# Seven of the K and V loads of a two-layer decode step are issued as three DMAs of 112, 8 and 8 rows

## The chip, the cores and the metric

The kernel runs on one core of a Trainium2 chip. The metric is the device time of one execution in microseconds (us). Of the kernel before, three runs are shown: 294.25, 294.75 and 295.55 us, so the median is 294.75 us. The profiled execution took 293.41 us, and its span in the profile is 291.6 us.

The core has five instruction streams that matter here: TensorE (PE, with its weight loads as PEld), VectorE (DVE), ScalarE (ACT), GpSimd (POOL) and SyncE (SP). SP computes nothing; it issues nearly all the DMAs. The data of a DMA is moved by the core's 16 DMA engines.

## The reference, cut to what matters

Two layers with the same weights and the same K and V caches are applied to four single-token rows `x` (batch 4, width 512, all bf16). Each layer is grouped-query attention followed by a gated MLP, each behind a layer norm without weights and each added to `x`:

```
q = (layernorm(x) @ wq) as 4 x 32 heads x 128          # 8 KV heads, 4 query heads on each
p = softmax(q . k_cache / sqrt(128))                   # k_cache: 4 x 8 x 4096 x 128
x = x + ((p . v_cache) @ wo)
h = sigmoid(layernorm(x) @ w_gate) * (layernorm(x) @ w_up)   # width 1792
x = x + h @ w_down
```

and the same again. K of one batch row and one KV head is 4096 x 128 in bf16, which is 1 MB, and V is the same. One layer reads 32 such K and 32 such V.

## The kernel before, in words

**Units and slots.** The work is cut into units: one layer, one batch row, one KV head. There are 64, and two neighbouring KV heads of one batch row form a pair. The string `ORDER` (line 118) writes out the order of the 32 pairs. The K or the V of a unit goes into a slot, an SBUF tile of 128 partitions with 8 KB in each. There are 14 slots (`NSLOT`), and four more when `wq` is no longer needed: `yield_wq` (line 1134) then gives its space away. Some K and V of the first layer stay in their slots for the second (`KEPT`), so 45 K and 49 V are loaded, each a load of 128 rows (one row for a partition, 8 KB). The last V alone is loaded as two halves of its columns.

**The order of the loads.** The string `LOADS` (line 122) writes out the order of all loads after `wq`, one letter for each: k and v for K and V, o for a piece of `wo`, g, u and d for the weights of the MLP. `loads` (line 333) is made from it, and `pump` (line 364) issues loads from its head on the queue of SP as long as a slot is free. SP waits, before each issue, until the last readers of the slot are done. A load raises the semaphore of its slot (`d0` to `d17`) by 16 when it has landed, and `S.last_write` of the slot's key (`s0` and so on) is what readers wait on.

**The work on a unit.** The string `PROGRAM` (line 126) writes out the order of all steps. `k_turn` (line 1142) transposes a landed K on VectorE in place; `scores` (line 1155) multiplies it with the queries on TensorE; `smax`, `spread_max`, `bias` and `expo` (lines 1187 to 1227) make the softmax; `ptrans` and `copies` turn the probabilities; `pv` (line 1323) multiplies them with V, and frees V's slot; `normalise` divides by the sums. Between the layers each batch row has a chain of 17 small steps (`pass_steps`, line 1088): the projection `wo`, the MLP and the queries of the second layer. After the last unit of the second layer comes the last MLP for all rows, and the output.

**What orders what.** Each engine runs its own list in the order written. Between engines `_Sched` (line 34) sets semaphore waits from the keys that a step reads and writes. A DMA is such a step: its token is counted in the order of the list, so that a wait on a later DMA of the same semaphore covers the earlier ones.

Of the kernel before, what the change touches and what calls it, by code (L numbers as in the profile page):

```python
# [119 lines left out]
111 113 133 131 130 132 122  # L120
"""
LOADS = """
ovkovookkk kkkuvkovkk vkovokovvg guddvkvkvv kkkvvkvvkk vkvvvvkkkv kvkkvkvvkv kvvkvkvkvv kvkvkkkvvk
vkvkvkvvvv kkkvvvvv
"""
PROGRAM = """
szmTbtpt snetzhbtuwmrpnPuiCtuuD sehtPzrtmpnaawtueawb szuatotDCuPiauuhabu
# [12 lines left out]
def bass_interleave_layers__gqa_block_cached__glu_gated_glu__decode_kernel(  # L140
# [17 lines left out]
    P = 128  # L158
# [19 lines left out]
    S = _Sched()  # L178
# [4 lines left out]
    def sbt(shape, dtype, name):  # L183
        cnt[0] += 1
        return es.enter_context(nc.sbuf_tensor(f"{name}_{cnt[0]}", list(shape), dtype))
# [27 lines left out]
    slot = [sbt([P, NJ * DH], dt.bfloat16, f"slot{i}") for i in range(NSLOT)]  # L213
# [110 lines left out]
    def loaded(kind, i):  # L324
        return seq[i][0] == 0 or not kept(kind, i)

    queue = {kind: [i for i in range(NU) if loaded(kind, i)] for kind in "kv"}
# [2 lines left out]
    queue["u"] = list(range(KD // 2))  # L330
    queue["d"] = list(range(2))
    kinds = {"k": "k", "v": "v", "o": "wo", "g": "wg", "u": "wu", "d": "wd"}
    loads = [(kinds[c], queue[c].pop(0)) for c in LOADS if not c.isspace()]
    assert not any(queue.values())
    loads.reverse()

# [24 lines left out]
    def take():  # L361
        return free.pop(0)

    def pump():
        while loads:
            kind, n = loads[-1]
            if kind in wparts:
                loads.pop()
                dst, src = wparts[kind](n)
                S.dma("sp", (lambda dst, src: lambda e: e.dma_start(dst, src))(dst, src), f"wo{n}" if kind == "wo" else kind, writes=[f"{kind}{n}"])  # L370
                continue
            if not free:
                return
            loads.pop()
            s = take()
            _, b, u = seq[n]
            if kind == "k":
                where["kn", n] = s
                src = A_k_cache[b, u].rearrange("(p j) d -> p (j d)", p=P)
            else:  # L380
                where["v", b, u] = s
                src = A_v_cache[b, u].rearrange("(p j) d -> p (j d)", p=P)
            parts = [(slot[s][:, :], src, f"d{s}", f"s{s}")]
            if kind == "v" and n == NU - 1:
                h = NJ * DH // 2
                parts = [(slot[s][:, 0:h], src[:, 0:h], "vh", "vh"), (slot[s][:, h:], src[:, h:], f"d{s}", f"s{s}")]
            for dst, frm, sem, key in parts:
                deps = S.readers.get(f"s{s}", []) + [S.last_write.get(f"s{s}")] if key == "vh" else ()
                S.dma(
                    "sp", (lambda dst, frm: lambda e: e.dma_start(dst, frm))(dst, frm), sem, writes=[key], deps=deps  # L390
                )
# [8 lines left out]
    for n in range(KD // 2):  # L400
# [4 lines left out]
            writes=[f"wq{2 * n}", f"wq{2 * n + 1}"],  # L405
        )
    pump()

    S.inst("pool", lambda e: e.memset(qz_sb[:, :, :, :, :], 0.0), writes=QZ + ["pf"])
# [6 lines left out]
        writes=["pe0"],  # L416
    )
    dve(lambda e: e.transpose(pidx[:, :], iota_f[:, 0:32]), writes=["pe0"])
    for a in range(4):
# [6 lines left out]
            writes=[f"ident{a}"],  # L426
# [5 lines left out]
    for k in range(KD):  # L432
# [13 lines left out]
        writes=[f"x{b}" for b in range(Bn)],  # L446
# [1183 lines left out]
    head_masks()  # L1630
    k_turn(0)
    pump()
    k_turn(1)
    pump()
    q_mm(Bn, 0, HQ)
    q_spread(0, Bn)
# [112 lines left out]
    for c in PROGRAM:  # L1749
# [29 lines left out]
        writes=["sel_row"],  # L1779
# [4 lines left out]
        writes=["rowk"],  # L1784
# [3 lines left out]
    for part in range(2):  # L1788
# [21 lines left out]
        writes=["o_row"],  # L1810
# [56 lines left out]
```

## Time and profile before

| | us |
|---|---|
| median of three runs (lowest, highest) | 294.75 (294.25, 295.55) |
| the profiled execution | 293.41 |
| its span in the profile | 291.6 |
| PE busy | 213.6 (73%) |
| DVE busy | 194.1 (67%) |
| ACT busy | 109.3 (37%) |
| POOL busy | 42.3 (15%) |

The span is the time between the first and the last instruction of the profiled execution. The page of the profile gives the busy time of each engine, then the span in 40 equal slices, then the DMA queues: for each queue the packets, the megabytes, and the time that its packets took as a share of 16 engines' span. A packet is one row of a load, or a completion mark of 4 bytes. Further views give the waits (who waited for whom, us in total, times, longest), the chain of work that ended last, the instructions in order of time, and the busy time of the engines in stretches of the span.

### The profile page before, as it was taken

The numbers are of one execution on the slowest core, as the hardware profiler recorded it, in microseconds if no ns is written. First come the engines' busy times: TensorE is split into PE (matmuls) and PEld (weight loads), VectorE is DVE, ScalarE is ACT, GpSimd is POOL, SyncE is SP. The second block draws the span as 40 slices with busy tenths as digits, with TensorE's granted clock in tenths as the row PEclk, the third lists the DMA queues.
The fourth block names the chain that finished last, engine by engine and source line by source line (L and its number), as shares of the span: only waits on it lengthen the run. The fifth ranks groups of instructions, "written<-read, shape, count | busy, mean of one in ns | idle before, by whom it ended". The sixth has DMA issues, their size and how long they took to land. (4 is left out here: it accounts for less than half of the span.)

```text
span 291.6 us, 10424 instructions
## 1 busy us (share of the span) xinstructions
PE 213.6 (73%) x4416; PEld 129.9 (45%) x4416; DVE 194.1 (67%) x498; ACT 109.3 (37%) x357; POOL 42.3 (15%) x213
## 2 busy tenths in 40 slices
PE   1130224666586886889988898999997899887895
PEld 1130101333336452455744454574564556463485
DVE  6420399876344866758789795868779595869443
ACT  2000114135330362653363554434646334566620
POOL 0000112202000121310011321001231200231100
PEclk9999999999997575755777555575555575766655
DMA  7999999999999999999999999999999999999900
GB/s 281 412 403 396 421 422 405 418 405 395 416 397 420 419 417 421 397 411 424 415 423 419 417 415 415 400 402 419 417 421 416 421 411 373 419 424 418 376 11 5
DMA packets 19781, 113.13 MB, mean 388 GB/s; under 512 B 1812, under 2 KB 5912, under 8 KB 7576
## 3 DMA queue, kind: packets, MB, share of 16 engines
q1 hardware_dynamic: 19712, 112.47, 94.5%
q8 instruction: 35, 0.57, 0.8%
q14 instruction: 10, 0.08, 0.1%
q10 hardware_dynamic: 24, 0.01, 0.0%
HBM read 112.46 MB, written 0.00 MB: 386 GB/s over the span
## 5 line engine op out<-in xcount | busy, mean ns | idle before, releaser
L1153 DVE STREAM_TRANSPOSE slot<-slot 128x1024 f32<-128x1024 f32 (+2 forms) x89 | 103.8, 1173 | 24.2 <-DMA slot<-in_A_k_cache_dram 23.3
L1290 ACT ACTIVATE pT<-PT 32x128 bf16<-32x128 f32 x232 | 62.0, 267 | 53.8 <-PE O_ps L1338 20.5
L1170 PE MATMUL S_ps<-slot,qz 128*16 128x512 bf16 x488 | 58.6, 597 | 10.6 <-DVE slot L1153 7.2
L1338 PEld LDWEIGHTS O_ps<-pT,slot 128*128 128x128 bf16 x1696 | 49.9, 102 | 28.5 <-ACT pT L1290 15.5
L1338 PE MATMUL O_ps<-pT,slot 128*128 128x4 bf16 x1696 | 54.1, 166 | 8.4 <-ACT pT L1290 6.8
L795 POOL COPY qz<-qs 32x32 bf16<-32x32 bf16 x112 | 22.8, 203 | 91.5 <-PE S_ps L1170 50.2
L1189 DVE TENSOR_REDUCE small_c<-S_ps 128x1 bf16<-128x512 f32 x32 | 21.7, 678 | 13.5 <-PE S_ps L1170 13.5
L1252 POOL TENSOR_TENSOR small_a<-small_b 128x8 bf16<-128x8 f32 x32 | 6.4, 199 | 137.0 <-ACT wide L1224 127.1
L1224 ACT ACTIVATE wide<-S_ps,small_b 128x512 bf16<-128x512 f32 x20 | 14.1, 705 | 23.3 <-DVE small_b L1217 19.3
L1170 PEld LDWEIGHTS S_ps<-slot,qz 128*16 128x16 bf16 x488 | 11.1, 103 | 26.3 <-issue 11.0
L1235 PE MATMUL PT<-ident_bf,wide 128*128 128x64 bf16 (+1 forms) x288 | 17.8, 221 | 3.4 <-ACT pT L1290 2.4
L1235 PEld LDWEIGHTS PT<-ident_bf,wide 128*128 128x128 bf16 x288 | 14.5, 118 | 8.5 <-issue 3.4
L1224 ACT ACTIVATE wide<-S_ps,small_b,small_a 128x512 bf16<-128x512 f32 x12 | 9.3, 778 | 12.9 <-DVE small_b L1217 5.1
L1399 PE MATMUL AC<-wo,oT 128*1 128x512 bf16 x96 | 11.7, 584 | 2.9 <-DVE oT L1373 2.9
L1197 PE MATMUL O_ps<-ident_bf,small_c 128*128 128x64 bf16 x32 | 7.0, 217 | 8.7 <-DVE small_c L1189 6.3
L747 PE MATMUL M_ps<-t_row,ident_bf 128*32 128x128 bf16 x16 | 0.6, 307 | 15.6 <-DVE t_row L730 15.6
L978 PE MATMUL M_ps<-wq,small_a 128*1 128x512 bf16 (+1 forms) x128 | 11.1, 510 | 0.6 <-DVE small_a L697 0.5
L758 ACT ACTIVATE qs<-M_ps 128x128 bf16<-128x128 f32 x4 | 0.8, 284 | 26.6 <-PE M_ps L747 26.6
L1197 PEld LDWEIGHTS O_ps<-ident_bf,small_c 128*128 128x128 bf16 x32 | 3.3, 104 | 14.9 <-DVE small_c L1189 8.9
L900 PE MATMUL M_ps<-wg,small_a 128*1 128x512 bf16 (+1 forms) x64 | 8.2, 556 | 1.6 <-DVE small_a L537 1.6
L925 PE MATMUL M_ps<-wu,small_a 128*1 128x512 bf16 (+1 forms) x64 | 9.1, 578 | 0.0
L1217 DVE TENSOR_REDUCE small_b<-O_ps 128x1 f32<-128x64 f32 x32 | 7.2, 225 | 2.8
(171 smaller groups left out, 241.6 us busy)
## 6 DMA issues: line engine op xcount, KB each, us to landing
slot<-in_A_v_cache_dram SPq DMA_DIRECT2D x47, 1024.0 KB, 9.8
slot<-in_A_k_cache_dram SPq DMA_DIRECT2D x42, 1024.0 KB, 11.1
wq<-in_A_wq_dram SPq DMA_DIRECT2D x2, 2048.0 KB, 10.2
wo<-in_A_wo_dram SPq DMA_DIRECT2D x8, 512.0 KB, 15.7
wq<-in_A_k_cache_dram SPq DMA_DIRECT2D x3, 1024.0 KB, 13.1
wu<-in_B_w_up_dram SPq DMA_DIRECT2D x2, 896.0 KB, 18.9
wg<-in_B_w_gate_dram SPq DMA_DIRECT2D x2, 896.0 KB, 14.2
wd<-in_B_w_down_dram SPq DMA_DIRECT2D x1, 1024.0 KB, 19.0
```

The costliest lines, as they stand in the source:

```text
L795: (lambda a, ps: lambda e: e.tensor_copy(qz_sb[ps, :, :, a, :], qs_sb[b][ps, :, c0:c0 + 2 * REP].rearrange("p t (u r) -> p u t r", r=REP), ...
L925: (lambda k, st, nt: lambda e: e.matmul(M_ps[1][32 * st:32 * st + 1, 0:nt * 2 * P], lhsT=xc_bf[:, k, 0:1], rhs=wv[:, k, bass.ds(st, nt, st ...
L978: (lambda k, st: lambda e: e.matmul(M[32 * st:32 * st + 1, 0:nj * P], lhsT=xc_bf[:, k, 0:1], rhs=q_rows[:, k, h, j0:j0 + nj, st, :], start ...
L1153: dve(lambda e: e.transpose(kf, kf), writes=[f"s{st}"])
L1170: (lambda t, b2, e_, c, ul, r0, ktv: lambda e: e.matmul(S_ps[p][r0:r0 + 4 * REP, :], lhsT=qz_sb[:, ul, t, :, :].rearrange("p a r -> p (a r)"),
L1189: dve(lambda e: e.tensor_reduce(rm_bf[:, 0:1], S_ps[p][:, :], AX.X, ALU.max), reads=[f"S{p}"], writes=["rmb"])
L1197: lambda e: e.matmul(O_ps[n][:, P:P + 64], lhsT=rm_bf[:, 0:1].broadcast_to([P, P]), rhs=valid_bf, start=True, stop=True),
L1224: lambda e: e.activation(pe_sb, S_ps[p][:, :], ACTF.Exp, bias=nm_sb, scale=scale, accum_out=sm_sb),
L1235: (lambda w, a0, a1, c0: lambda e: e.matmul(PT[:, c0:c0 + 16 * (a1 - a0)], lhsT=wide_sb[:, NV + 64 * w:NV + 64 * w + P], rhs=valid_bf[:, : ...
L1290: (lambda dst, frm: lambda e: e.activation(dst, frm, ACTF.Copy))(dst, frm),
L1338: (lambda n, x, c, j: lambda e: e.matmul(bank[:, ul * REP:(ul + 1) * REP], lhsT=vv[:, x * JG + c * 4 + j, :], rhs=pT[:, x % 2, j, x // 2, ...
L1399: (lambda r, h, i: lambda e: e.matmul(AC[32 * r:32 * r + 1, :], lhsT=oT_sb[:, h, own_column:own_column + 1], rhs=wo_sb[:, h, :], start=(j ...
```

## The change

In `LOADS` seven letters become capitals: three k and four v. They are the letters 43, 55, 64, 73, 84, 94 and 106 of 108. The list `loads` gets a third entry that tells whether the letter was a capital, and `pump` issues such a load as three DMAs on SP, one behind the other: rows 0 to 111, rows 112 to 119 and rows 120 to 127. Only the first of them waits for the slot's earlier readers. All three raise the semaphore of the slot by 16, and the key's last write is the third, so readers wait for all three. The other 87 loads of K and V, the data in the slots, the order of the loads and all other steps stay as they are.

```diff
 LOADS = """
-ovkovookkk kkkuvkovkk vkovokovvg guddvkvkvv kkkvvkvvkk vkvvvvkkkv kvkkvkvvkv kvvkvkvkvv kvkvkkkvvk
-vkvkvkvvvv kkkvvvvv
+ovkovookkk kkkuvkovkk vkovokovvg guddvkvkvv kkKvvkvvkk vkvvVvkkkv kvkKvkvvkv kvVkvkvkvv kvkVkkkvvk
+vkvKvkvvvv kkkvvVvv
 """
@@
-    loads = [(kinds[c], queue[c].pop(0)) for c in LOADS if not c.isspace()]
+    loads = [(kinds[c.lower()], queue[c.lower()].pop(0), c.isupper()) for c in LOADS if not c.isspace()]
@@
-            kind, n = loads[-1]
+            kind, n, uneven = loads[-1]
@@
+            if uneven:
+                whole = None
+                for rows in (slice(0, P - 16), slice(P - 16, P - 8), slice(P - 8, P)):
+                    whole = S.dma(
+                        "sp", (lambda d, f: lambda e: e.dma_start(d, f))(slot[s][rows, :], src[rows, :]), f"d{s}",
+                        writes=() if whole else [f"s{s}"],
+                    )
+                S.last_write[f"s{s}"] = whole
+                continue
```

## The prediction

> **What bounds the kernel now.** I read the page's head, slices and DMA queues first, then the chain, then waits and stretches.
>
> ```profile
> span 291.6 us, 10424 instructions
> PE 213.6 (73%) x4416; PEld 129.9 (45%) x4416; DVE 194.1 (67%) x498; ACT 109.3 (37%) x357; POOL 42.3 (15%) x213
> ...
> DMA  7999999999999999999999999999999999999900
> GB/s 281 412 403 396 421 422 405 418 405 395 416 397 420 419 417 421 397 411 424 415 423 419 417 415 415 400 402 419 417 421 416 421 411 373 419 424 418 376 11 5
> ...
> q1 hardware_dynamic: 19712, 112.47, 94.5%
> q8 instruction: 35, 0.57, 0.8%
> q14 instruction: 10, 0.08, 0.1%
> q10 hardware_dynamic: 24, 0.01, 0.0%
> ```
>
> The DMA engines are full in every slice until 277 us, and no compute engine is. The best slices move about 420 GB/s, so a load of 1.049 MB takes 2.50 us; each of the 16 engines moves 8 of its 128 rows, so a row costs an engine 2.50 / 8 = 0.31 us. Besides the loads there are 35 packets of instructions: 0.8% of 16 x 291.6 us is 37.3 us of one engine's time, 1.07 us a packet.
>
> ```profile
> 229.56 10.75 DMA slot<-in_A_v_cache_dram
> 240.31 0.05 issue
> 240.36 1.00 PE O_ps L1338 x32
> ...
> 249.68 0.33 SPq L390
> 250.00 0.05 issue
> 250.06 11.11 DMA wq<-in_A_k_cache_dram
> 261.16 0.02 issue
> 261.18 2.31 DVE wq L1153
> ```
>
> This is the chain that ended last. It holds two loads, 10.75 and 11.11 us from issue to landing, that is four loads deep in the queue; between and behind them it is compute. Nothing waits for the last load of all: the chain's end is set by when the K load of 250.06 is whole. How close compute runs beside this:
>
> ```profile
> 125.00:180.00 55.00, 48.58 (x992) 28.74 (x984) 41.40 (x108) 26.95 (x88) 9.89 (x49) 0.59 1.01 419
> 180.00:200.00 20.00, 18.93 (x380) 11.54 (x384) 15.55 (x54) 7.38 (x24) 2.61 (x13) 0.59 0.99 401
> 200.00:236.00 36.00, 32.52 (x642) 18.92 (x630) 27.86 (x66) 18.24 (x60) 7.64 (x38) 0.50 1.01 420
> ```
>
> The columns are the stretch, its length, the busy time of PE, PEld, DVE, ACT, POOL, the granted clock and the DMA share. From 200 to 236 us PE is busy for 32.52 of 36 us at a clock of 0.50, beside a DMA share of 1.01. Two resources are nearly full, and the waits between them are short:
>
> ```profile
> PEld O_ps L1338 <- DMA slot<-in_A_v_cache_dram: 0.8, 1, 0.8
> ...
> DVE wq L1153 <- DMA wq<-in_A_k_cache_dram: 1.2, 1, 1.2
> ```
>
> The first is the only wait for a load in 180 to 240 us, the second the longest from 240 us on. They stand where the chain has its two DMA pieces (240.3 and 261.2 us). So an earlier landing is worth at most about 0.8 us at the first, and 1.2 us more at the second, beyond which compute sets the time.
>
> **What the change does to the engines.** It moves rows between DMA engines. How many engines a part uses can be counted from packets and issues:
>
> ```profile
> slot<-in_A_v_cache_dram SPq DMA_DIRECT2D x47, 1024.0 KB, 9.8
> slot<-in_A_k_cache_dram SPq DMA_DIRECT2D x42, 1024.0 KB, 11.1
> wq<-in_A_wq_dram SPq DMA_DIRECT2D x2, 2048.0 KB, 10.2
> wo<-in_A_wo_dram SPq DMA_DIRECT2D x8, 512.0 KB, 15.7
> wq<-in_A_k_cache_dram SPq DMA_DIRECT2D x3, 1024.0 KB, 13.1
> wu<-in_B_w_up_dram SPq DMA_DIRECT2D x2, 896.0 KB, 18.9
> wg<-in_B_w_gate_dram SPq DMA_DIRECT2D x2, 896.0 KB, 14.2
> wd<-in_B_w_down_dram SPq DMA_DIRECT2D x1, 1024.0 KB, 19.0
> wq<-in_A_v_cache_dram SPq DMA_DIRECT2D x1, 1024.0 KB, 8.5
> slot<-in_A_v_cache_dram SPq DMA_DIRECT2D x2, 512.0 KB, 22.8
> wd<-in_B_w_down_dram SPq DMA_DIRECT2D x1, 768.0 KB, 20.5
> out_dram<-slot SPq DMA_DIRECT2D x2, 1.0 KB
> out_dram<-slot ACTq DMA_DIRECT2D x2, 1.0 KB
> t_row<-in_A_x_dram ACTq DMA_DIRECT2D x1, 4.0 KB
> ```
>
> ACT's queue q10 carries three DMAs of 4 rows (x, two quarters of the output): 12 rows, but 24 packets, so each left 4 completion marks, one for each engine used. SP's queue q1 carries 111 loads over 128 partitions and two quarters of the output. Their contiguous pieces are 12,160 (K and V), 256 (wq), 4,096 (wo), 512 (wu, wg), 896 (wd) and 8: 17,928. The other 19,712 - 17,928 = 1,784 packets are marks: 16 for each load, 4 for each quarter. So 4 rows use 4 engines and 128 rows use 16. Of 8 rows the trace has no example; between these rows they use 8, one row on each. Then 112 rows put 7 rows on each of 16 engines, and the two parts of 8 rows put 2 more on the same eight: 9 rows on eight engines, 7 on the others, where it was 8 and 8. Seven such loads move 7 x 0.31 = 2.2 us of work from each of eight engines to each of the other eight. Bytes in all stay the same.
>
> [...]
>
> **Who has room.** A load is whole when its slowest engine is done. If the 37.3 us of instruction packets fell evenly on 16 engines (2.3 us each), the rows would be even now and the change would make them uneven. If they fall on eight engines, these carry 37.3 / 8 = 4.7 us more than the rest; over the span they are the late ones, and the moved work closes 2 x 2.2 = 4.4 of the 4.7 us. Call s the share of the packets on the eight engines that lose rows. The slowest set gets lighter only if s x 4.7 exceeds (1 - s) x 4.7 + 2.2, that is s above 0.73. The trace's completion marks, which no view prints one by one, show the engines of most loads in two sets of eight, an early and a late one, and instruction packets hitting the late set in turn. I take it that the set is eight. That it is the set which loses rows no row says, and the 0.23 below stands for that.
>
> **The sum.** At a DMA share of 0.99 to 1.01 the late engines hardly run dry, so what is taken from them counts in full until compute binds. By count of letters, the V load at 229.56 us is the 93rd, with five split loads ahead of it; the K load at 250.06 us is the 101st, with six.
>
> - First DMA piece: the late engines finish 5 x 0.31 = 1.55 us earlier; the wait there was 0.8 us, so the chain gains 0.8 us and compute binds.
> - Second piece: issue comes 0.8 us earlier. The late engines are 6 x 0.31 = 1.86 us ahead, and DVE, which waited 1.2 us, is free 0.8 us earlier: 2.0 us is there to gain, 1.86 us is taken.
> - Behind it, 30 us of compute shift as they are. The last V, with seven split loads up to it, comes 2.2 us earlier, so no new wait appears.
>
> Together -1.86 us. Against that, what is added:
>
> ```profile
> 229.56 0.33 SPq L390 DMA_DIRECT2D slot<-in_A_v_cache_dram  x1
> 229.94 0.43 SPq L390 DMA_DIRECT2D slot<-in_A_k_cache_dram  x1
> ...
> SPq L106 <- PE O_ps L1338: 94.5, 33, 8.0
> SPq L106 <- PE S_ps L1170: 34.0, 10, 6.0
> ```
>
> Fourteen more issues at 0.33 to 0.43 us are 4.6 to 6.0 us of SP's time. Of a split load itself the last part is issued 0.66 to 0.86 us later, and so is what stands behind it. SP waits 94.5 + 34.0 us for slots and the queue is 10 us deep, so I cost this at nothing; where the queue is dry it would cost up to 0.86 us for that load. The fourteen small parts bring 14 x 8 more completion marks, 4 bytes each; q10's 24 packets round to 0.0%, so nothing. The parts have no wait of their own: only the first waits for the slot, as the whole load did, and readers wait for all three.
>
> The profiled execution would go from 293.41 to 291.55 us (span 289.7). That execution is 1.34 us below the median of the runs shown, so on the median it is 294.75 - 1.86 = 292.9 us; I say 293.0. The full 2.2 us would be 292.6; a tenth of the best case lies below, since the runs scatter by 0.8 us above the median and 0.5 us below it: low end 291.8.
>
> **The rivals.**
>
> *Compute takes the gain.* PE at 32.52 of 36 us, at half clock, speaks for it: if the chain's first DMA wait goes and PE is bound by its own list, and at 261 us DVE is held by the scores before, only the 0.8 us at the first piece stay, or nothing. Against it: the second piece still ends on a load, with 1.2 us of wait. 294.75 - 0.8 = 293.95, and 294.75 if nothing stays. Chance 0.24.
>
> *The wrong eight get the rows (slower).* The eight engines that take two rows more are those that carry the instruction packets, or the late set is spread over both halves. One mechanism: the late engines have no idle time, so every row moved to them makes the landings later. At 240.3 us it is 5 x 0.31 = 1.55 us, at 261.2 us 1.86 us, and 2.2 us at the end: 294.75 + 1.9 to 2.2 = 296.6 to 296.9. It decides when s is below 0.73. For it: no row names the set. Against it: only that the sizes fit (4.4 moved against 4.7). Chance 0.23.
>
> *Small parts cost their own latency (slower).* A part of 64 KB ends with a completion of its own; if SP or the queue runs dry just there, 0.86 us for each such load. Two of them on the path give 294.75 + 1.7 - 0.8 = 295.7 at most. The GB/s line speaks against it: slices with the 512 KB pieces of wo and slices of 1 MB loads both move 395 to 424. Chance 0.03, within 0.5%.
>
> [...]
>
> *The parts do not split that way.* If 8 rows went to all 16 engines or to another eight each time, the load stays even and the time is 294.75. It is part of the 0.24.
>
> **How the numbers follow.** Forecast 0.50 (293.0, own range 291.8 to 293.9), compute or no effect 0.24 (293.95 to 294.75), wrong eight 0.23 (296.6 to 296.9), small parts 0.03. Half a per cent is 1.47 us, about what a measurement of this kernel can tell from no change. Faster by more than that (below 293.28): 0.48, most of the forecast and a little of the second case. Slower (above 296.22): 0.24. Between: 0.28. To leave out no more than two in ten the range has to reach into the wrong-eight case: 291.8 to 296.9.
>
> **What would show it.** Right: in the chain the DMA pieces end earlier (the K piece near 259.3 us) and the two waits for loads in 180 to 292 us shrink; GB/s stays near 420 in slices that now read 397 to 411; issue to landing is shorter at the median. Compute case: the waits go, the DMA share falls below 1, and SP's wait for PE grows. Wrong eight: the same slices fall, and waits of DVE and PE on slot loads grow beyond 0.8 and 1.2 us. The number of packets of q1 tells the engines: seven split loads with 8 + 8 marks beside 16 add 112 packets (19,824 in all); 16 marks each would make 19,936. The prediction fails if s is below 0.73, or if compute is nearer to the chain than the two waits say.

## The result, and the profile after

The change made the kernel slower by 9%: 323.04 us median (six runs, 319.99 to 328.2) against 294.98 us (six runs), ratio 1.090 with a 95% interval of 1.083 to 1.096. Two of the six runs (327.73 and 328.2 us) fell in a slower state and the ratio leaves them out, so it stands for a loss of some 26 us, where the two medians are 28 us apart. Either lies far outside the forecast range (291.8 to 296.9 us), on the slow side. The two profiled executions, which the rows below come from, took 293.41 and 323.5 us and are 30.1 us apart.

The page of the changed kernel, head, slices and the queue of the loads:

```profile
span 321.7 us, 10438 instructions
PE 214.5 (67%) x4416; PEld 130.3 (41%) x4416; DVE 195.0 (61%) x498; ACT 109.2 (34%) x357; POOL 42.3 (13%) x213
...
DMA  7999999999999999999999999999899999999930
GB/s 298 405 394 411 423 411 413 407 395 418 397 421 414 312 364 419 416 335 260 421 404 220 377 414 294 295 409 423 288 302 344 404 308 279 380 413 394 243 137 5
...
q1 hardware_dynamic: 19824, 112.47, 95.2%
```

Compute is what it was (PE 214.5 against 213.6 us, DVE 195.0 against 194.1 us), and so are the bytes. The DMA line is as full as before. But the GB/s line has seven dips, from slice 14 on, one for each split load. DMA engines that are busy as before and move little more than half the bytes are nearly the whole result. In stretches (columns as in the prediction; the last two are DMA share and GB/s), the seven dips and two stretches between them:

```profile
108.00:115.00 7.00, 3.85 (x91) 2.58 (x91) 4.42 (x5) 2.43 (x9) 0.60 (x3) 0.51 1.00 235
141.00:151.00 10.00, 8.96 (x212) 5.99 (x208) 6.33 (x26) 5.38 (x20) 1.95 (x10) 0.67 1.03 235
168.00:179.00 11.00, 7.88 (x169) 4.42 (x157) 6.05 (x15) 5.02 (x17) 2.62 (x13) 0.50 1.02 235
197.00:208.00 11.00, 7.89 (x170) 5.16 (x166) 5.83 (x23) 3.49 (x11) 0.60 (x3) 0.66 1.02 264
230.00:241.00 11.00, 5.54 (x120) 3.03 (x112) 5.81 (x10) 3.17 (x12) 2.82 (x14) 0.66 1.00 288
260.00:271.00 11.00, 7.47 (x162) 4.82 (x153) 5.85 (x10) 1.39 (x6) 0.09 (x1) 0.66 0.99 243
296.00:305.00 9.00, 6.24 (x153) 4.17 (x149) 4.07 (x10) 6.02 (x20) 2.05 (x11) 0.68 1.02 243
115.00:141.00 26.00, 22.29 (x386) 11.74 (x385) 18.14 (x47) 10.53 (x32) 5.04 (x25) 0.50 1.01 418
179.00:197.00 18.00, 13.27 (x256) 7.51 (x254) 11.99 (x31) 6.50 (x21) 3.02 (x15) 0.50 1.00 402
```

At a DMA share of 0.99 to 1.03 the dips move 235 to 288 GB/s; between them it is 402 to 418. In the first six of these stretches the kernel before moves 415 to 422 GB/s. Against 420 GB/s the seven stretches lose 7 x (1 - 235/420) = 3.1 us, then 4.4, 4.8, 4.1, 3.5, 4.6 and 3.8 us, together 28.3 us. It is an estimate, since the ends of the stretches are chosen by eye, and it covers 28.3 of the 30.1 us between the two profiled executions. A dip is longer than one load: 7 to 11 us, while a split load at full speed would take 2.5 us. It holds 1.6 to 3.2 MB, more than the 1.05 MB of one load, so whole loads beside it in the queue are slow too.

The waits (us in total, times, longest) show the loss arriving at compute, DVE at K and PE at V:

```profile
DVE slot L1162 <- DMA slot<-in_A_k_cache_dram: 44.1, 18, 9.7
...
PE O_ps L1347 <- DMA slot<-in_A_v_cache_dram: 17.2, 8, 5.1
...
PEld O_ps L1347 <- DMA slot<-in_A_v_cache_dram: 15.9, 7, 5.2
```

Before, the first two of these waits were:

```profile
DVE slot L1153 <- DMA slot<-in_A_k_cache_dram: 23.3, 10, 8.4
...
PE O_ps L1338 <- DMA slot<-in_A_v_cache_dram: 0.7, 2, 0.5
```

### The profile page after: what moved, and what is told of

The parts are those of the page before. It is cut to its first block, busy times and chain, and to the rows that moved or that the text cites. A ratio compares the mean times of both kernels' runs of the same rounds, so it can differ in the third digit from the quotient of the medians.

```text
span 321.7 us, 10438 instructions
## 1 busy us (share of the span) xinstructions
PE 214.5 (67%) x4416; PEld 130.3 (41%) x4416; DVE 195.0 (61%) x498; ACT 109.2 (34%) x357; POOL 42.3 (13%) x213
## 3 DMA queue, kind: packets, MB, share of 16 engines
q1 hardware_dynamic: 19824, 112.47, 95.2%
## 5 line engine op out<-in xcount | busy, mean ns | idle before, releaser
L1179 PE MATMUL S_ps<-slot,qz 128*16 128x512 bf16 x488 | 57.8, 591 | 13.9 <-DVE slot L1162 7.2
L1382 DVE TENSOR_TENSOR oT<-O_ps,small_a 128x8 bf16<-128x8 f32 (+1 forms) x32 | 5.1, 161 | 12.7 <-PE O_ps L1347 11.8
```

The source lines that it names most:

```text
L1179: (lambda t, b2, e_, c, ul, r0, ktv: lambda e: e.matmul(S_ps[p][r0:r0 + 4 * REP, :], lhsT=qz_sb[:, ul, t, :, :].rearrange("p a r -> p (a r)"),
```

## The experiments

Three theories, made from the result. *Small parts*: each extra DMA costs time of its own. *Wrong eight*: 9 rows on some engines and 7 on others make the loads late. *Alignment*: the 112-row part deals partitions to engines so that engines collide (two write the same few partitions at one time), and every row in flight takes near twice its 0.31 us. The time is measured: the 201 rows of 8 KB that start from 108 to 115 us took 0.57 us at the median, 0.31 us before. The collision is a guess: no view shows which engine writes which partition.

**Three parts by columns.**

```diff
-for rows in (slice(0, P - 16), slice(P - 16, P - 8), slice(P - 8, P)):
-    ... slot[s][rows, :], src[rows, :]
+for cut in (slice(0, 3584), slice(3584, 3840), slice(3840, 4096)):
+    ... slot[s][:, cut], src[:, cut]
```

> The same seven loads are issued as three DMAs, but cut by columns: 128 rows of 7168, 512 and 512 bytes, so every engine keeps its 8 partitions. Alignment theory (the 112-row part gives each engine 7 neighbouring partitions, engines collide, and every row in flight takes near twice its 0.31 us): 295 us, within 0.5% of before. Small-parts theory (two extra small DMAs per load cost about 4 us each load, by latency and completions): 310 us or more. Wrong-eight theory (9 and 7 rows are the cost): 295 us.

Measured: 294.97 us, ratio 1.000 (0.997 to 1.003). Three DMAs on one semaphore, two of them of 64 KB, cost nothing that can be measured. The small-parts theory falls. What costs is the cut by rows. Whether an engine has the same 8 partitions in all three parts, as the expectation takes it, no view shows.

**Even shares: 112 and 16 rows.**

```diff
-for rows in (slice(0, P - 16), slice(P - 16, P - 8), slice(P - 8, P)):
+for rows in (slice(0, P - 16), slice(P - 16, P)):
```

> Two parts by rows, 112 and 16: 7 rows and then 1 row on each of 16 engines, so the shares are even again and one small part fewer. Alignment theory: still 315 to 325 us, since the 112 rows stay as they are. Small-parts theory: about half the loss, 305 to 310 us. Wrong-eight theory: back to 295 us.

Measured: 320.84 us (two runs, 318.14 and 323.53, too few for an interval). By 16 marks for each part (112 packets more in all, 19,824) each engine has 8 rows again, and the loss stays (23 and 29 us in the two runs), so the wrong eight can't be its cause.

**Two halves.**

```diff
+for rows in (slice(0, P // 2), slice(P // 2, P)):
```

> Two halves of 64 rows each, 4 rows on each of 16 engines, no small part, even shares. Alignment theory: slower than before too, since the 16 engines write 64 partitions at a time and not 128; if a row takes twice its time for the load, 7 x 2.5 = 17 us, so 305 to 315 us. Small-parts and wrong-eight theories: 295 us.

Measured: 324.37 us, ratio 1.101 (1.092 to 1.110). The loss comes without any odd share: a cut into two blocks of neighbouring partitions is enough. My size for it (17 us) was too small; the loss is 29 us.

**Is it the source or the destination?** Two runs read the same rows in the same order, even ones and then odd ones. One writes them to the even and the odd partitions, the other to partitions 0 to 63 and 64 to 127, so that in the second the rows of these loads stand in another order than the reference's.

```diff
+for rows in (slice(0, P, 2), slice(1, P, 2)):            # first run
+    ... slot[s][rows, :], src[rows, :]
+for half in range(2):                                    # second run
+    ... slot[s][half * 64:half * 64 + 64, :], src[half::2, :]
```

> Two parts of 64 rows as before, but of the even and of the odd rows: each part writes partitions over all of SBUF, and reads every second row. The sum is as the reference's. If the destination partitions cause the slow rows, this differs clearly from the two halves (324 us): two engines still meet on neighbouring partitions but can get out of each other's way, so 300 to 318 us. If the source's addresses cause them, it is as the run with the spread source. If any cut by rows costs the same, 324 us.

> Two parts of 64 rows that write partitions 0 to 63 and 64 to 127, as the two halves did, but read the even and the odd rows; the rows of these seven K and V so stand in another order, and the result is not the reference's. If the destination causes the slow rows: 324 us, as the two halves. If the source's addresses do: it differs from 324 us, and equals the even and odd rows' run.

Measured: 294.83 us, ratio 1.001 (0.996 to 1.006), for the even and odd partitions; 323.33 us, ratio 1.096 (1.090 to 1.103), for the halves. The GB/s line of the first, and then of the second:

```profile
GB/s 282 408 407 392 422 420 408 420 399 397 419 395 420 412 413 418 381 420 420 355 423 423 418 421 405 401 387 420 420 421 418 419 408 387 419 425 420 364 7 5
```

```profile
GB/s 302 407 394 411 421 412 415 406 396 414 399 421 417 307 353 421 416 314 258 418 419 217 370 417 278 314 419 419 296 323 382 416 273 248 408 422 373 246 106 3
```

The same bytes are read in the same order; only the partitions written differ, and the dips come and go with them. It is the destination. But the cut into even and odd partitions is not just better than blocks: it is free, which I had not expected (300 to 318 us).

**Blocks of 16, and every eighth row.**

```diff
+for rows in [slice(16 * n, 16 * n + 16) for n in range(8)]:   # first run
+for rows in [slice(n, P, 8) for n in range(8)]:               # second run
```

> The seven loads as eight parts of 16 neighbouring rows, one row on each engine. If the cost is that engines meet on the same few partitions, 16 neighbours are worse than 64: with twice the time of a row at 64 rows, four times or so here, 1.2 us a row, 10 us a load, 7 x 7.5 = 52 us more, 335 to 350 us. If every cut into blocks costs the same, 324 us. If the number of DMAs sets the cost: above 340 us, and the strided run too.

> The same eight parts of 16 rows, but each takes every eighth row, so that its 16 rows lie over all partitions. If the engines' meeting on the same partitions is the cause: as before, 294 to 298 us, with up to 2 us for 49 more issues. If the number of DMAs or their size is the cause: as the blocks of 16.

Measured: 325.74 us, ratio 1.104 (1.092 to 1.115), for the blocks, and 323.5 us, ratio 1.096 (1.087 to 1.105), for every eighth row. The collision theory as I had it failed in both runs: it gave 335 to 350 us and 294 to 298 us. Of the other cases that I had named, the blocks cost what any cut into blocks costs (324 us), and every eighth row costs what the blocks do, which I had kept for a cost by the number or the size of the DMAs. The number alone had been given above 340 us. Narrower blocks are no worse than halves within the intervals, so the loss doesn't grow as the blocks get narrower. And parts that lie over all of SBUF can be as slow as blocks. "Spread over the partitions" is thus not the condition.

**Every fourth row.** The load queue has 112 packets more with two parts of 64 rows (19,824) and 784 more with eight parts of 16 (20,496), 16 marks for each further part. Dealt evenly to 16 engines, a whole load gives an engine 8 rows and a part of every second row 4; both were free. A part of every eighth row gives it one, and was slow. Every fourth row lies between, with 2 rows for an engine.

```diff
+for rows in [slice(n, P, 4) for n in range(4)]:
```

> The seven loads as four parts of 32 rows, each taking every fourth row (0, 4, 8 ..., then 1, 5, 9 ...). [...] Theory that a part has to give an engine at least 4 rows: slow as every eighth row, 315 to 325 us. [...]

Measured: 294.61 us, ratio 1.003 (0.999 to 1.006). The page of this run, slices and queue:

```profile
GB/s 279 411 407 393 422 421 409 413 406 394 417 398 421 416 410 415 394 422 425 413 417 419 420 417 410 401 409 422 419 419 417 419 404 358 414 423 420 389 10 5
...
q1 hardware_dynamic: 20048, 112.47, 94.7%
```

No dip, with 2 rows for an engine and 21 more DMAs (20,048 - 19,712 = 336 marks, 16 for each). So neither a share of 2 rows nor a stride by itself is slow, and the theory of at least 4 rows falls. What is left is which cuts are free (columns, every second, every fourth row) and which are slow (112, 8 and 8, 112 and 16, halves, blocks of 16, every eighth row). Why the partitions that a part writes set its speed, no run shows.

One rival has no run of its own. A part of 16 rows gives an engine one row, and each such part here (blocks of 16, every eighth row, the 16 of 112 and 16) stood in a slow cut; other sets of 16 rows were not tried. One row for an engine can't be the whole cause, though: the halves, with 4 rows for an engine, lose as much (1.101).

**One split load.**

```diff
-the capitals at letters 55, 64, 73, 84, 94 and 106
+small letters there; only letter 43 stays a capital
```

> Only the first of the seven loads (letter 43) is issued as 112, 8 and 8 rows. If each split load costs the same: 28 / 7 = 4.0 us, so 299 us. If the loss comes from splits that meet one another or from the end of the kernel: 295 to 296 us.

Measured: 298.34 us, ratio 1.010 (1.006 to 1.014), that is 2.9 us, within 1.8 to 4.0. In stretches around that load and behind it:

```profile
108.00:116.00 8.00, 4.23 (x91) 2.53 (x91) 4.18 (x6) 2.02 (x7) 0.69 (x4) 0.50 1.00 224
116.00:140.00 24.00, 20.28 (x369) 11.38 (x369) 16.33 (x41) 9.75 (x30) 4.94 (x25) 0.50 1.01 418
140.00:151.00 11.00, 10.25 (x216) 6.60 (x210) 7.18 (x28) 5.15 (x18) 1.20 (x6) 0.50 1.00 408
```

One dip, 8 x (1 - 224/420) = 3.7 us at full weight, and 408 GB/s where the second dip was. The loss comes with each split load by itself: seven times 2.9 us is 20 us, and seven times the upper 4.0 us is 28 us. The trace's packet records, which no view prints, show it row by row. From 108 to 115 us every one of the 187 rows of 8 KB took over 0.4 us, 0.57 us at the median; before, 358 rows took 0.31 us. From 105 to 118 us 232 rows were that slow. The split load has 128, so at least 104 are rows of the loads around it. Why those slow down too, with their rows over all partitions, no run shows.

**Did the eight engines have room?** The loads are whole again, and behind each of the seven two parts of 8 rows are copied from memory to a scratch in memory.

```diff
+S.dma("sp", ... slot[s][:, :], src, f"d{s}", writes=[f"s{s}"])
+for r in (P - 16, P - 8):
+    S.dma("sp", ... spill[n:n + 8, :], src[r:r + 8, :], "spill")                    # first run
+    S.dma("sp", ... spill[n:n + 8, 0:4080], src[r:r + 8, 0:4080], "spill")          # second run
```

> The seven loads are whole again, and behind each two parts of 8 rows are copied in addition, from the K or V in memory to a scratch in memory, which nothing reads. 14 x 8 more rows of 8 KB on eight engines (if 8 rows use eight engines), 4.4 us per engine, nothing taken from the others. Alignment theory: 295 us if these eight engines are the early ones with room, 297 to 299 us if they are the late ones. Small-parts theory: 310 us or more, since 14 small DMAs are still there. Wrong-eight theory: 299 us or more.

> As in the run with extra rows, but 8160 of each row's 8192 bytes are copied, so that the rows stay apart and can't be joined: 14 x 8 packets of 8160 bytes and, if 8 rows use eight engines, 14 x 8 marks, so q1 has 19,936 packets. Those eight engines carry 4.3 us more than before, the others nothing more. If the eight are the early ones, within 0.5% of before (294 to 296 us). If they are the late ones, up to 4.3 us more at the end, 297 to 299 us. If the loads' landing sets the time only in part, the second case is nearer to 296.5 us.

The queue of the loads in the first run, and in the second:

```profile
q1 hardware_dynamic: 20160, 113.39, 94.7%
```

```profile
q1 hardware_dynamic: 19936, 113.38, 94.8%
```

The first isn't the test it was meant to be: it has 20,160 - 19,712 = 448 packets more, 32 for each copy, not 16. The 8 contiguous rows were joined and cut into 16 pieces of 4 KB (224 more packets of 2 to 8 KB than before, 16 for each copy) over all 16 engines, with 16 marks. It so measures something else: 0.92 MB more, 2.2 us of each engine, cost 0.24% (-0.1 to 0.6), some 0.7 us. In the second the count is as expected, 16 for each copy, so eight engines carry 4.3 us more if each copy uses the same eight, and the kernel took 297.72 us, ratio 1.009 (1.006 to 1.012), 2.6 us. Eight early engines with 4.7 us of room would have hidden that. So the engines that 8 rows use here, if they are always the same eight, are not eight with that much room. Whether they are the late eight, or some late and some early ones, these runs don't tell.

**9 and 7 rows without blocks.**

```diff
+for rows in (slice(0, P, 2), slice(1, P, 4), slice(3, P, 8), slice(7, P, 16), slice(15, P, 16)):
```

> The seven loads give 9 rows to eight engines and 7 to the others, as the change does, but no part is a block of neighbouring partitions: 64 even rows, 32 rows (1, 5, 9 ...), 16 rows (3, 11 ...), 8 rows (7, 23 ...) and 8 rows (15, 31 ...). The sum is as the reference's. If the eight engines are the early ones, as I forecast: 293 to 294 us. If they are the late ones: 297 us. If half of them are late ones: 295.5 to 297 us. If any unequal split slows the rows: 310 us or more.

Measured: 303.77 us, ratio 1.028 (1.023 to 1.034), 8.4 us more. The 64 and the 32 rows are free kinds of part; the 16 rows (one an engine) are of the slow kind, as in the run with every eighth row, and whether the two parts of 8 (two more on eight engines, if both use the same) are too, no run shows. In the run with every eighth row, 8 rows an engine in seven loads cost 28 us, 0.5 us for each; here 1 to 3 rows for each load would cost 3.5 to 10.5 us. The 8.4 us lie in between. The trace shows where they are:

```profile
109.00:113.00 4.00, 2.62 (x71) 1.91 (x75) 3.15 (x3) 1.33 (x5) 0.57 (x3) 0.50 1.01 291
142.00:146.00 4.00, 3.85 (x115) 3.68 (x115) 2.25 (x10) 0.00 (x0) 0.00 (x0) 0.50 0.98 283
166.00:171.00 5.00, 4.29 (x102) 2.60 (x100) 3.56 (x8) 2.89 (x10) 1.97 (x10) 0.50 1.02 293
190.00:194.00 4.00, 3.79 (x47) 1.33 (x41) 3.45 (x10) 2.80 (x9) 0.40 (x2) 0.65 1.02 283
220.00:225.00 5.00, 3.79 (x70) 1.79 (x67) 3.52 (x7) 3.02 (x10) 1.04 (x6) 0.50 1.02 295
247.00:251.00 4.00, 3.16 (x96) 2.87 (x100) 2.67 (x5) 0.00 (x0) 0.00 (x0) 0.50 1.00 274
279.00:284.00 5.00, 4.37 (x67) 1.87 (x64) 2.08 (x6) 3.57 (x13) 0.60 (x3) 0.50 1.03 315
```

There are seven dips again, shorter ones, at a full DMA share. Against 420 GB/s they lose 1.2, 1.3, 1.5, 1.3, 1.5, 1.4 and 1.3 us, together 9.5 us, which covers the 8.4 us. So the dips account for the loss, and no cost of shares of 9 and 7 is to be seen beside them. Neither cut with 9 and 7 rows ran without dips, and no kernel of this study was faster than the one before.

## Why the prediction was wrong, point by point

**The failed step** is in "What the change does to the engines", where a row was moved at its price of before: "7 x 0.31 = 2.2 us of work", with "bytes in all stay the same". I took the time of a row, 0.31 us, as a property of the engine. It depends on which partitions a part writes: around the one load cut into 112, 8 and 8 rows, a row took 0.57 us at the median, 1.8 times as long, those of the neighbouring whole loads too. At some 4 us for each of seven loads these slow stretches come to 28.3 of the 30.1 us between the profiled executions. That the runs show; the cause of it they don't. None of my rivals had it: I looked at how many rows an engine gets, and not at which.

**How many engines a part uses**: right. q1 has 19,824 packets, the number given for 8 + 8 + 16 marks. But the 9 and 7 rows, and with them the 2.2 us, also need both parts of 8 rows to fall on the same eight engines in every load; no run shows that, only the 8 marks for each part.

**Small parts at no cost**: right. The columns run has the same number of DMAs and is at 1.000. Nor does the number of DMAs set the loss: with the 112 and 16 rows there are 7 extra DMAs and the loss is 23 to 29 us, with the columns 14 and none.

**Who has room**: wrong as far as it can be tested. I took the eight engines that gain rows to be early, on the fit of 4.4 against 4.7 us. Copies with 8 marks each cost 2.6 us. Nor do the completion marks, which I had read as two sets of eight, show sets that lie 4.7 us apart: in the packed trace of the kernel before, the 16 marks of a load lie 2.05 us apart from first to last at the median and 3.6 us at most, and the widest gap between neighbouring marks falls between the 8th and the 9th in 7 of 111 loads. So the change would probably not have paid even with rows at 0.31 us, though no run shows that; and the wrong eight is no part of the loss to be seen here, since even shares lose as much.

**The worth of DMA time on the path**: probably too high. I let 1.86 of 2.2 us through to the end. 2.2 us more on every engine cost 0.7 us (at most 1.8), so some of such a change seems to stay in the slack between load and use.

**What would show it**: I had named the slices falling and the waits for slot loads growing as the sign of the wrong eight. Both came, from another cause. The line that tells them apart is the 235 GB/s beside a DMA share of 1.00. With the copies of 8 rows beside whole loads, by estimate 4.3 us more on eight engines, no slice falls like that: the lowest from the second to the 38th is 362 GB/s, where the kernel before has 373.

## What to carry to other kernels

In the kernel before, a load over all 128 partitions took an engine 0.31 us a row. Cutting such a load by columns, or by every second or fourth row, was free here (ratios 1.000, 1.001 and 1.003); cutting it into blocks of neighbouring rows (112 and 16, 64 or 16), or by every eighth row, cost about 4 us for each of seven 1 MB loads (2.9 us where only one was split, into 112, 8 and 8; at least 104 rows of the whole loads around it were slow too). When a change moves work between units that run side by side, ask what the new dealing touches (here which partitions a part writes), and not only how even it is. A resource can be full and move little more than half of what it did (here 235 GB/s at a DMA share of 1.00, where 419 were moved before): read busy share and GB/s together.

## What the runs showed of the hardware that I had not expected

Cutting a 1 MB load into parts of every second row (ratio 1.001) or every fourth (1.003) costs nothing, while parts of every eighth row cost as much as blocks (1.096 against 1.104 for blocks of 16 and 1.101 for halves): the loss did not grow with narrower blocks. One split load slowed at least 104 rows of the loads around it. And 8 rows that are contiguous on both sides, memory to memory, ran on all 16 engines (32 packets a copy), while the same rows with 32 bytes left out of each ran on eight (16 packets).
